# A decode-attention kernel bound by its load stream: the first weight load moved ahead of the opening barrier, the closing barrier dropped, four tiny side loads added

## The chip, the cores and the metric

One core of a Trainium2 chip runs the whole program; the other cores are idle. The metric is the time of one execution in microseconds of device time, the median of several executions. Runs of one experiment alternate on one chip with runs of the kernel before, so a kernel is compared with the kernel before of the same rounds. The profiled span (first to last instruction) is 1.3 to 2.1 us shorter than the time; the rest lies after the last instruction or before the first. A load is shared by 16 DMA engines: "first engine" and "last engine" below are the first and the last of them to land their share. A "packet" is one record of the trace, in the large loads one partition's row. In profile lines, PEld is TensorE's weight load, and a q after an engine's name is the sequencer that issues its instructions.

## The reference, cut to what matters

```python
B, Sq, D = 4, 1, 448
Hq, Hkv, Sk, Dh = 16, 8, 8192, 256          # all bfloat16
# k_cache, v_cache: (4, 8, 8192, 256), 134 MB each

x  = A_x
xn = _layernorm(x)
s  = attention(xn, k_cache, v_cache, wq, wo)  # one query token, 2 query heads per K/V head
g  = silu(_B_ref(xn, w1, w2, w3, w4))         # a small MLP on the same four rows
return x + s * g
```

There are 32 pairs of batch and K/V head ("heads" below). Each needs 4 MB of K and 4 MB of V once, so nearly all of the 279 MB that are read are read once and used once.

## The kernel before: the parts that matter

SyncE (SP) issues the whole load stream on one queue; ScalarE (ACT) issues the small x load.

```python
def prog_sp(sp):
    sp.dma_start(vflat[1][:, 0:DK * HDH], A_wq...).then_inc(S["dwq"], 16)   # 3.67 MB, 28,672 bytes a partition
    sp.dma_start(vflat[0][:, 0:DK * FH],  B_w3...).then_inc(S["dw3"], 16)
    sp.dma_start(w4_sb...,                B_w4...).then_inc(S["dw4"], 16)

    def load_k(h):
        if h >= 2:
            sp.wait_ge(S["v_k"], h - 1)       # K buffer h%2 free: K of body(h-2) is transposed and copied out
        sp.dma_start(kn_dst(h), A_k_cache[b, g]...)                         # 4 MB, 32,768 bytes a partition
    def load_v(h):
        ...
            sp.wait_ge(S["v_v"], h + 1)       # V buffer h%2 free
            sp.dma_start(vflat[h % 2], ...)

    load_k(0)
    load_k(1)
    load_wo(NLATE, HQ, "dwo")                 # 2.75 MB: the last load that waits for no buffer
    for h in range(2, NH):
        load_k(h)                             # load_k(2), "the third K load", waits for body(0)
        load_v(h - 2)
    load_v(NH - 2)
    load_v(NH - 1)                            # in four pieces
    for i, hs in enumerate(LATE):
        load_wo(hs[0], hs[-1] + 1, "dwl%d" % i)   # three late pieces of the output weights, 0.9 MB
    sp.wait_ge(S["v_out"], 1)
    store(sp, 0)
    take(sp, "dout", 16 * NDG)                # wait until the output has landed

def prog_act(act):
    act.dma_start(x_sb[:, :], x2d).then_inc(S["dx"], 16)    # 4 rows of 896 bytes
    ...
```

The prologue is a chain that begins at x: cast to float32, two layernorms (VectorE), transposes, the query projection with wq, the MLP with w3 and w4, then 14 warm-up matmuls (TensorE). Only then TensorE begins body(0):

```python
for i in range(NWARM):                        # NWARM = 14
    pe.matmul(psv[0:PVW, 0:QW], pT[:, 0, 0:PVW], wq_sb[:, 0, 0:QW], start=True, stop=True)
... body(0): transposes of K 0, scores, ...   # its last copied transpose frees the K buffer for load_k(2)
```

Ahead of all this the framework puts four constants on GpSimd and a barrier over all engines, and a barrier closes the program.

Of the kernel before, what the change touches and what calls it, by code (L numbers as in the profile page):

```python
# [10 lines left out]
BF16 = dt.bfloat16  # L11
# [6 lines left out]
class _Chain:  # L18
# [9 lines left out]

    def sync(self):
        self.eng.wait_ge(self.sem, self.n)  # L30


def bass_recurrent_scan__gqa_block_cached__mixer_s_mlp__decode_kernel(
# [12 lines left out]
):  # L46
    Bn, Sq, D = A_x.shape
    _, HKV, SK, DH = A_k_cache.shape
    HD = A_wq.shape[1]
    HQ = HD // DH  # L50
# [3 lines left out]
    NHF = 2  # L54
    DK = D * NHF // P
    assert D * NHF == DK * P and DK % 2 == 1 and D == DK * (P // 2)
    HDH, FH = HD // NHF, F // NHF
# [11 lines left out]
    NH = Bn * HKV  # L69
# [30 lines left out]
    def where(h):  # L100
        return Bn - 1 - h // HKV, h % HKV

    with ExitStack() as es:
        def sb(name, shape, dty):
            return es.enter_context(nc.sbuf_tensor(name, shape, dty))
# [43 lines left out]
        bout = sb("bout", [DP, DQ], F32)  # L149
        out_b = sb("out_b", [DP, DQ], BF16)  # L150
        st = sb("st", [Bn, 16], F32)

        pst = [es.enter_context(nc.psum_tensor("pst%d" % i, [P, 512], F32)) for i in range(NST)]
        psc = [es.enter_context(nc.psum_tensor("psc%d" % i, [P, 512], F32)) for i in range(2)]
# [1 line left out]
        psv = es.enter_context(nc.psum_tensor("psv", [P, 512], F32))  # L156

        S = {n: es.enter_context(nc.semaphore(n)) for n in (
            ["dx", "dwq", "dw3", "dw4", "dwo", "dk0", "dk1", "dv0", "dv1", "dout"]
            + ["dvl%d" % i for i in range(NPIECE)] + ["dwl%d" % i for i in range(len(LATE))]  # L160
            + ["p_td", "p_ta", "p_sc", "p_m1", "p_m2", "p_m3", "p_tr", "p_ou", "p_pv", "p_x", "p_q", "p_h", "p_h2", "p_o"]
            + ["v_ev", "a_ev", "v_rmax", "v_diag", "v_neg", "v_ot", "a_exp", "g_q", "g_c",
# [3 lines left out]
        vflat = [vb[:, i].rearrange("p c d -> p (c d)") for i in range(2)]  # L166
# [17 lines left out]
        def kn_dst(h):  # L184
            return kn[:, h % 2].rearrange("p c d -> p (c d)")

        def store(eng, i):
            eng.dma_start(out2d[:, i * DQ:(i + 1) * DQ], out_b[i * PQ:i * PQ + Bn, :]
                          ).then_inc(S["dout"], 16)

        def prog_sp(sp):
            sp.dma_start(vflat[1][:, 0:DK * HDH],
                         A_wq.rearrange("d (t n) -> (d t) n", t=NHF).rearrange(
                             "(p j) n -> p (j n)", j=DK)).then_inc(S["dwq"], 16)
            sp.dma_start(vflat[0][:, 0:DK * FH],
                         B_w3.rearrange("d (t n) -> (d t) n", t=NHF).rearrange(
                             "(p j) n -> p (j n)", j=DK)).then_inc(S["dw3"], 16)
            sp.dma_start(w4_sb.rearrange("p a k n -> p a (k n)"),
                         B_w4.rearrange("(a p k) n -> p a (k n)", a=NHF, k=NFK)
                         ).then_inc(S["dw4"], 16)  # L200

            def load_k(h):
                b, g = where(h)
                if h >= 2:
                    sp.wait_ge(S["v_k"], h - 1)
                sp.dma_start(kn_dst(h), A_k_cache[b, g].rearrange("(p c) d -> p (c d)", p=P)
                             ).then_inc(S["dk%d" % (h % 2)], 16)

            def load_v(h):
                b, g = where(h)  # L210
                src = A_v_cache[b, g].rearrange("(p c) d -> p c d", p=P)
                if h < NH - 1:
                    sp.wait_ge(S["v_v"], h + 1)
                    sp.dma_start(vflat[h % 2], src.rearrange("p c d -> p (c d)")
                                 ).then_inc(S["dv%d" % (h % 2)], 16)
                else:

                    sp.wait_ge(S["v_k"], h)
                    for i in range(NPIECE):
                        lo, hi = PIECES[i], PIECES[i + 1]  # L220
                        sp.dma_start(
                            kn[:, 1 - h % 2, lo:hi, :].rearrange("p c d -> p (c d)"),
                            src[:, lo:hi, :].rearrange("p c d -> p (c d)")
                        ).then_inc(S["dvl%d" % i], 16)

            load_k(0)
            load_k(1)
            wo_src = A_wo.rearrange("(h p c) n -> p h (c n)", p=P, c=NHALF)

            def load_wo(lo, hi, sem):  # L230
                sp.dma_start(wo_sb[:, lo:hi].rearrange("p h c n -> p h (c n)"),
                             wo_src[:, lo:hi]).then_inc(S[sem], 16)

            load_wo(NLATE, HQ, "dwo")
            for h in range(2, NH):
                load_k(h)
                load_v(h - 2)
            load_v(NH - 2)
            load_v(NH - 1)
            for i, hs in enumerate(LATE):  # L240
                load_wo(hs[0], hs[-1] + 1, "dwl%d" % i)
            sp.wait_ge(S["v_out"], 1)
            store(sp, 0)
            take(sp, "dout", 16 * NDG)

        def take(eng, name, n=1):
            eng.wait_ge(S[name], n).then_inc(S[name], -n)  # L247
# [285 lines left out]
        def prog_pe(pe, xn_mark, xn2_mark):  # L533
# [224 lines left out]
            with nc.Fori(0, 2, engines=[e]) as part:  # L758
# [3 lines left out]
                with pe.If(part == 1):  # L762
                    finish()

        block = es.enter_context(nc.Block())
        marks = []

        @block.sync
        def _(eng):
            prog_sp(eng)  # L770
# [13 lines left out]
        @block.tensor  # L784
        def _(pe):
            prog_pe(pe, *marks)


# [26 lines left out]
```

## Time and profile before

| | |
|---|---|
| time | 655.11 us median (654.53 to 656.17, 4 runs) |
| profiled span | 653.1 us |
| bytes read | 278.99 MB, 427 GB/s over the span |

Lines of the profile page of the kernel before. The digits give busy tenths in 40 slices of 16.3 us; the last line is the load queue: packets, MB, share of 16 engines' span.

```profile
span 653.1 us, 22864 instructions
...
PE   1898997988888988888897887898788798888897
...
DMA  8999999999999999999999999999999999999996
GB/s 362 444 421 421 443 421 446 421 444 423 444 423 444 421 446 421 446 421 446 421 443 423 442 425 442 425 442 425 438 429 438 429 438 429 434 434 434 434 424 288
...
q1 hardware_dynamic: 12328, 278.99, 99.3%
...
```

The load queue takes 99.3% of the DMA engines' time; TensorE is busy for 85% of the span. The kernel is bound by its load stream. In the landing records of the trace two heads (16.78 MB) land every 38.73 us, which is 433 GB/s.

The waits of SP, before (who waits, for whom, us in total, times, longest):

```profile
...
SPq L206 <- DVEq L502: 458.8, 30, 38.6
SPq L214 <- DVEq L471: 133.8, 31, 20.2
...
SPq L247 <- SPq L247: 1.1, 1, 1.1
...
SPq L103 <- SPq L103: 0.5, 1, 0.5
```

The first two lines are waits for free buffers, which cost nothing as long as loads are still queued. The line L247 is the wait for the output's landing, and L103 the closing barrier: 0.5 us.

The head of the program, from the timeline of the kernel before (start, duration, engine, line, operation; in brackets the idle time before and what ended it):

```profile
...
0.73 0.58 ACTq L300 DMA_DIRECT2D x_sb<-in_A_x_dram  x1
...
0.74 0.41 SPq L192 DMA_DIRECT2D vb<-in_A_wq_dram  x1
...
2.57 1.97 DVE L373 CAST x_f<-x_sb 4x448 f32<-4x448 bf16 x1 [1.16 <-DMA x_sb<-in_A_x_dram]
...
25.57 4.52 PE L582 MATMUL psv<-vb,pT 128*32 128x512 bf16 x14
...
30.03 1.07 PE L590 MATMUL pst<-ident_b,kn 128*128 128x128 bf16 x16
...
42.56 0.33 SPq L206 DMA_DIRECT2D kn<-in_A_k_cache_dram  x1
...
```

x is issued at 0.73 us and wq at 0.74. The first K load lands at 29.47 us.

The stretches around the third K load, before (stretch, length, busy us and count per engine, granted clock, DMA share, GB/s). Packets are long here, and a share above 1.00 in a short stretch means that they reach over its edge.

```profile
core 0: us, PE busy (x) PEld busy (x) DVE busy (x) ACT busy (x) POOL busy (x), PEclk, DMA share, GB/s
30.00:44.00 14.00, 13.16 (x275) 12.08 (x274) 6.49 (x12) 7.65 (x11) 0.00 (x0) 1.00 0.97 399
44.00:50.00 6.00, 5.96 (x114) 4.68 (x109) 3.43 (x8) 2.70 (x7) 0.19 (x1) 1.00 1.14 478
...
```

### The profile page before, as it was taken

The numbers are of one execution on the slowest core, as the hardware profiler recorded it, in microseconds if no ns is written. First come the engines' busy times: TensorE is split into PE (matmuls) and PEld (weight loads), VectorE is DVE, ScalarE is ACT, GpSimd is POOL, SyncE is SP. The second block draws the span as 40 slices with busy tenths as digits, with TensorE's granted clock in tenths as the row PEclk, the third lists the DMA queues.
The fourth block names the chain that finished last, engine by engine and source line by source line (L and its number), as shares of the span: only waits on it lengthen the run. The fifth ranks groups of instructions, "written<-read, shape, count | busy, mean of one in ns | idle before, by whom it ended". The sixth has DMA issues, their size and how long they took to land. (4 is left out here: it accounts for less than half of the span.)

```text
span 653.1 us, 22864 instructions
## 1 busy us (share of the span) xinstructions
PE 552.8 (85%) x9937; PEld 473.5 (73%) x9937; DVE 276.1 (42%) x589; ACT 256.2 (39%) x364; POOL 13.5 (2%) x77
## 2 busy tenths in 40 slices
PE   1898997988888988888897887898788798888897
PEld 0487886986676887667787775797677688766785
DVE  7443554343344443434443443434344344443442
ACT  4153543443334443323443342444234344332340
POOL 2000000000000000000000000000000000000000
PEclk9798999888789878889987798989779987888999
DMA  8999999999999999999999999999999999999996
GB/s 362 444 421 421 443 421 446 421 444 423 444 423 444 421 446 421 446 421 446 421 443 423 442 425 442 425 442 425 438 429 438 429 438 429 434 434 434 434 424 288
DMA packets 12354, 279.13 MB, mean 427 GB/s; under 512 B 1205, under 2 KB 3257, under 8 KB 3769
## 3 DMA queue, kind: packets, MB, share of 16 engines
q1 hardware_dynamic: 12328, 278.99, 99.3%
q8 instruction: 7, 0.11, 0.1%
q10 hardware_dynamic: 16, 0.01, 0.0%
q14 instruction: 3, 0.02, 0.0%
HBM read 278.99 MB, written 0.00 MB: 427 GB/s over the span
## 5 line engine op out<-in xcount | busy, mean ns | idle before, releaser
L590 PE MATMUL pst<-ident_b,kn 128*128 128x128 bf16 x4096 | 345.8, 238 | 77.8 <-PEq L247 76.0
L297 ACT ACTIVATE kT<-pst 128x1024 bf16<-128x1024 bf16 x224 | 229.5, 1025 | 357.6 <-ACTq L247 356.7
L590 PEld LDWEIGHTS pst<-ident_b,kn 128*128 128x128 bf16 x4096 | 274.7, 108 | 83.4 <-issue 82.9
L295 DVE COPY kT<-pst 128x1024 bf16<-128x1024 bf16 x288 | 197.5, 692 | 260.9 <-DVEq L247 260.9
L602 PE MATMUL psc<-qc,kT 128*128 128x2 bf16 x4096 | 178.0, 164 | 0.8 <-issue 0.8
L602 PEld LDWEIGHTS psc<-qc,kT 128*128 128x128 bf16 x4096 | 156.7, 98 | 29.5 <-issue 29.1
L641 PE MATMUL psv<-vb,pT 128*4 128x512 bf16 x1056 | 86.3, 378 | 0.4 <-issue 0.4
L620 PE MATMUL psm<-sel,po 128*128 128x2 f32 x272 | 36.7, 257 | 0.5 <-PEq L247 0.5
L620 PEld LDWEIGHTS psm<-sel,po 128*128 128x128 f32 x272 | 34.7, 196 | 0.9 <-issue 0.9
L641 PEld LDWEIGHTS psv<-vb,pT 128*4 128x4 bf16 x1056 | 22.2, 82 | 15.4 <-issue 0.9
L454 DVE TENSOR_REDUCE rmax<-psc 128x2 f32<-128x128 f32 x32 | 9.3, 292 | 48.9 <-DVEq L247 48.9
L472 DVE COPY po<-psv 128x512 f32<-128x512 f32 x34 | 23.5, 692 | 3.0 <-DVEq L247 2.3
L459 DVE TENSOR_REDUCE gmax<-psm 2x1 f32<-2x128 f32 x32 | 8.9, 279 | 34.7 <-DVEq L247 34.7
L319 ACT ACTIVATE pT<-psc,negb 128x64 bf16<-128x64 f32 x66 | 20.6, 333 | 5.4 <-ACTq L247 5.4
L614 PEld LDWEIGHTS psm<-diag,ones_f 2*128 2x128 f32 x66 | 13.9, 260 | 6.4 <-issue 5.4
L282 POOL COPY qc<-qT 128x4 bf16<-128x4 bf16 x32 | 6.0, 188 | 583.3 <-DVEq L471 565.8
L614 PE MATMUL psm<-diag,ones_f 2*128 2x2 f32 x66 | 16.6, 319 | 1.1 <-PEq L247 0.9
L319 ACT ACTIVATION_READ_ACCUMULATOR pT<-psc,negb 128x1 f32 x66 | 13.6, 206 | 0.0
L610 PEld LDWEIGHTS psm<-ident_f,rmax 128*2 128x2 f32 x32 | 2.6, 80 | 14.0 <-issue 14.0
L538 PE MATMUL pst<-ident_b,xn_b 4*128 4x4 bf16 x14 | 0.6, 161 | 13.6 <-DVE xn_b L367 8.9
L632 PE MATMUL psm<-rowsum,ones_f 128*128 128x2 f32 x64 | 11.6, 251 | 0.0
L538 PEld LDWEIGHTS pst<-ident_b,xn_b 4*128 4x128 bf16 x14 | 0.5, 98 | 13.6 <-issue 8.9
(101 smaller groups left out, 119.3 us busy)
## 6 DMA issues: line engine op xcount, KB each, us to landing
kn<-in_A_k_cache_dram SPq DMA_DIRECT2D x32, 4096.0 KB, 25.2
vb<-in_A_v_cache_dram SPq DMA_DIRECT2D x31, 4096.0 KB, 30.5
vb<-in_A_wq_dram SPq DMA_DIRECT2D x1, 3584.0 KB, 11.3
vb<-in_B_w_dram SPq DMA_DIRECT2D x2, 1568.0 KB, 16.2
wo_sb<-in_A_wo_dram SPq DMA_DIRECT2D x1, 2688.0 KB, 43.2
kn<-in_A_v_cache_dram SPq DMA_DIRECT2D x1, 2048.0 KB, 24.9
kn<-in_A_v_cache_dram SPq DMA_DIRECT2D x1, 1024.0 KB, 26.9
kn<-in_A_v_cache_dram SPq DMA_DIRECT2D x2, 512.0 KB, 28.0
```

The lines of the kernel that those rows point to most:

```text
L295: engine.tensor_copy(dst, src).then_inc(S["v_ev"], 1)
L297: engine.activation(dst, src, ACT.Copy).then_inc(S["a_ev"], 1)
L319: ins = act.activation(pv_p[:, :, hh], sc[:, :, hh], ACT.Exp, bias=negb[:, s, hh:hh + 1], scale=SCALE, accum_out=rowsum[:, s, hh:hh + 1])
L454: v.tensor_reduce(rmax[:, :], psc[h % 2][:, 0:NCH * REP].rearrange("p (k h) -> p h k", h=REP), AX.X, ALU.max).then_inc(S["v_rmax"], 1)
L459: v.tensor_reduce(gmax[:, :], psm[0:REP, 0:P], AX.X, ALU.max).then_inc(S["v_s"], 1)
L472: v.tensor_copy(po[:, slot], psv[:, 0:CP * DH]).then_inc(S["v_po"], 1)
L590: ins = pe.transpose(dst[:, t * P:(t + 1) * P], kn[:, h % 2, GC * j + kl, half * P:(half + 1) * P], ident_b[:, :])
L602: ins = pe.matmul(psc[h % 2][:, kk * REP:(kk + 1) * REP], kT[:, j % RING, t * P:(t + 1) * P], qc[:, h % 2, half, :], start=(half == 0), st ...
L614: pe.matmul(psm[:, P:P + REP], ones_f[0:REP, :], diag[:, :], start=True, stop=True).then_inc(S["p_m2"], 1)
L620: ins = pe.matmul(dst(dh)[:, 0:width], po[:, slot, i * DH + dh:(i + 1) * DH:NHALF], sel[:, i, 0:width], start=(i == 0), stop=(i == CP - 1))
L632: pe.matmul(psm[:, P + REP:P + 2 * REP], ones_f[:, :], rowsum[:, h % 2, :], start=True, stop=True)
L641: ins = pe.matmul(psv[o:o + CP * REP, 0:CP * DH], pT[:, h % 2, kk * REP:(kk + CP) * REP], src[:, kk:kk + CP, :].rearrange("p c d -> p (c d)"),
```

## The change

The intent: begin the stream earlier by the length of the opening barrier, end the program without the closing barrier, and put four side loads (15 rows of 64 bytes, never used) into the middle of the stream.

```diff
+def begin_ahead(nc, loads):          # moves the named instructions in front of SP's first barrier instruction
+    ...
+    blocks[0].instructions = first[:at] + list(loads) + first[at:]
+
+def drop_end_barrier(nc):
+    nc.main_func.blocks[-1].instructions = []
...
+        aside = sb("aside", [8, 4, 32], BF16)
...
-            sp.dma_start(vflat[1][:, 0:DK * HDH],
-                         A_wq...).then_inc(S["dwq"], 16)
+            ahead.append(sp.dma_start(
+                vflat[1][:, 0:DK * HDH], A_wq...).then_inc(S["dwq"], 16))
...
             for h in range(2, NH):
                 load_k(h)
                 load_v(h - 2)
+                if h == NH // 2 + 4:
+                    for i in range(4):
+                        n = 1 << i
+                        sp.dma_start(aside[0:n, i, :], A_wo[0:n, 0:32]).then_inc(S["das"], 16)
...
             store(sp, 0)
+            sp.wait_ge(S["das"], 64)
             take(sp, "dout", 16 * NDG)
...
+    begin_ahead(nc, [a.ins for a in ahead])
+    drop_end_barrier(nc)
```

## The prediction

> **What bounds the kernel now.** The load stream. The page's DMA part shows 99.3% of 16 engines' span spent in packets of the one load queue, 278.99 MB at a mean 427 GB/s; TensorE is busy 85%, VectorE 42%, ScalarE 39%. In the trace's landing records, two heads (16.78 MB) land every 38.73 us from about 55 us to 628 us, which is 433 GB/s without a gap, and nearly every 32,768-byte packet takes 1,213 ns. The Trainium skill, "DMA: Bandwidth & Descriptors", Specifications, gives 435 GB/s as the fabric ceiling; the trace agrees. SP waits for free buffers (458.8 us for K, 133.8 us for V), but loads land 25 to 30 us (median) after issue against 9.7 us per transfer, so work is always queued. The tail also hangs on the stream: the last weight load's 16 engines land between 647.6 and 649.8 us, the last matmuls end at 650.3, the store is issued at 651.13, and the span ends at 653.1.
>
> So what moves the first packet moves the end.
>
> **First load ahead of the opening barrier.** In the timeline SP's first instruction is at 0.0; the barrier releases SP at 0.66 and the weight load is issued at 0.74, its first packet starting at 1.77. Issued first, it starts about 0.7 us earlier. It takes SP 0.41 us, and the barrier is held by GpSimd's constants until 0.53, so the barrier does not move. The other loads are issued as before. The stream has no later slack to absorb the shift: the first buffer-dependent K load is issued at 42.6 us, 4 us before the queue would run dry. Gain: 0.7 us. The small x load (896-byte packets at 1.7 us) will queue behind 28,672-byte packets, up to about 1 us later; the layernorm chain has slack, since the first K lands at 29.5.
>
> **No closing barrier.** SP's wait for the stores ends at 663.56 on the trace's clock, the last barrier instruction at 664.09: 0.52 us, all on the end of the path. Gain: 0.5 us, unless what follows the program waits in another way.
>
> **Side loads.** Fifteen rows of 64 bytes. By the skill, same page, "Why a DMA increments its semaphore by 16 and not by 1", a DMA of k rows uses the lowest-numbered k engines, so one engine gets four rows, most get one or none; this trace has no engine numbers. A 448-byte packet took 22 ns and a semaphore packet 9 ns, so I estimate at most 4 x 31 = 0.12 us on one engine, likely not the last. Issuing costs SP about 4 x 0.4 us near 402 us, inside a wait that lasts until 419. Cost: 0 to 0.1 us. I see no gain: every engine's large packets are already back to back.
>
> **Prediction.** 655.15 - 0.7 - 0.5 + 0.05 = 654.0 us; 80% range 653.0 to 655.0. Faster by over 2%: 0.01; within 2%: 0.98; slower by over 2%: 0.01.
>
> **Right if** the first load packet starts near 1.0 us, all landings are about 0.7 us earlier to the end, the cadence stays at 38.73 us, the spread of landings over the engines (2.2 us at the end) keeps its size, and nothing but the stores' landing ends the span, near 651.9.
>
> **Wrong if** the early issue delays the barrier or its packets start no sooner; if the side loads cost a stall (a cadence step after 400 us) or change the spread among engines; if what runs after the program takes back the 0.5 us; or if an added instruction fetch lands on the last engine.

## More of the kernel before

The cast of x ends at 4.54. The warm-up matmuls begin at 25.57, body(0) at 30.03, and when its last transpose has been copied SP issues the third K load, at 42.56.

## The result

655.89 us median (655.8 to 656.29, 4 runs), against 655.11 before. The ratio of the means is 1.0011 (95% interval 0.9998 to 1.0024): the same at 2%, as forecast, but the 1.2 us that were to be gained are not there, and the time lies outside the range of 653.0 to 655.0. Ratios are the mean time of one kernel's runs over that of the other's of the same rounds, so not quite the ratio of the medians quoted.

The page of the changed kernel:

```profile
span 654.4 us, 22857 instructions
...
DMA  9999999999999999999999999999999999999996
GB/s 381 450 365 425 432 431 439 435 433 433 433 433 435 433 433 433 433 433 433 433 432 431 435 431 435 435 433 435 431 435 433 435 431 441 427 441 429 437 423 289
...
q1 hardware_dynamic: 12358, 278.99, 99.2%
...
```

The third number of the GB/s line (32.7 to 49.1 us) says it first: 365 GB/s, where before had 421. The timeline of the head, after:

```profile
...
0.00 0.39 SPq L214 DMA_DIRECT2D vb<-in_A_wq_dram  x1
...
0.80 0.57 ACTq L328 DMA_DIRECT2D x_sb<-in_A_x_dram  x1
...
6.74 0.38 DVE L401 CAST x_f<-x_sb 4x448 f32<-4x448 bf16 x1 [5.26 <-DMA x_sb<-in_A_x_dram]
...
28.15 4.83 PE L610 MATMUL psv<-vb,pT 128*32 128x512 bf16 x14
...
32.91 1.07 PE L618 MATMUL pst<-ident_b,kn 128*128 128x128 bf16 x16
...
44.43 0.33 SPq L229 DMA_DIRECT2D kn<-in_A_k_cache_dram  x1
...
```

wq is issued at 0.00 instead of 0.74, as intended. x is issued at 0.80, but its cast begins at 6.74, after 5.26 us of waiting for x to land. Everything behind it is late by 2.6 us: the warm-up begins at 28.15 instead of 25.57 and body(0) at 32.91 instead of 30.03. The third K load is issued at 44.43 instead of 42.56.

Two accidents of the profiled run before blur these differences. x landed 4.2 us later, but its cast only ended 2.6 us later, because in the run before the cast took 1.97 us and here 0.38; what stretched it there is not shown. And body(0) took 15.62 us before and 14.61 here, because TensorE paused in it before (0.84 us idle) and not here; more on this pause below. Without that pause the third K load would have been later by 2.9 us and not by 1.87.

The same stretches, after:

```profile
core 0: us, PE busy (x) PEld busy (x) DVE busy (x) ACT busy (x) POOL busy (x), PEclk, DMA share, GB/s
30.00:44.00 14.00, 14.00 (x247) 11.92 (x246) 5.45 (x12) 7.58 (x11) 0.00 (x0) 1.00 1.00 409
44.00:50.00 6.00, 5.77 (x99) 3.72 (x97) 3.24 (x8) 1.09 (x2) 0.19 (x1) 1.00 0.88 328
...
```

In the stretch from 44 to 50 us the DMA share falls from 1.14 to 0.88. The waits of SP, after:

```profile
...
SPq L229 <- DVEq L530: 459.7, 30, 41.1
SPq L237 <- DVEq L499: 132.4, 31, 18.9
...
SPq L275 <- SPq L275: 1.2, 1, 1.2
SPq L831 <- PEq L831: 0.2, 1, 0.2
```

The closing barrier's line is gone.

Where the time went, from the landing and packet records of the two profiled runs:

| | before, us | after, us | difference |
|---|---|---|---|
| first packet of wq starts | 1.77 | 1.02 | -0.75 |
| packets of x start | 1.69 to 2.17 | 5.03 to 5.29 | +3.2 |
| x has landed | 2.55 | 6.71 | +4.2 |
| cast of x ends | 4.54 | 7.12 | +2.6 |
| last load ahead of the third K: first engine lands | 44.98 | 44.28 | -0.70 |
| third K load is issued | 42.56 | 44.43 | +1.87 |
| idle time of the 16 engines, 44 to 50 us | none | 20.2 (1.26 each) | |
| third K: first engine, last engine lands | 54.65, 56.39 | 55.88, 58.06 | +1.23, +1.67 |
| last K (head 31) has landed | 618.34 | 619.54 | +1.20 |
| body(31), its first transpose to the transpose of its row maxima | 16.15 | 17.05 | +0.90 |
| store is issued | 651.13 | 652.93 | +1.80 |
| last instruction ends | 653.10 | 654.38 | +1.28 |

The gain of the head is there until 44 us, and it is given back, and more, where the third K load comes. There are 1.26 us of idle time per engine, and the first packets of the third K load take 1.2 to 2.5 us instead of 1.21, which is 0.62 us per engine more. Together with the -0.70 that makes +1.18 for the first engine; +1.23 was measured. That the last K comes +1.20 later is not the same number carried through: the last engine is 1.7 us behind up to head 16 and about 1.2 from head 17 on, because there, near 330 us, the kernel before loses 0.4 to 0.5 us on its last engine and the changed one does not. Two instruction fetches run near 330 us in both; why only one loses by it is not shown.

### The profile page after: what moved, and what is told of

It is laid out like the page before. It is cut to its first block, busy times and chain, and to the rows that moved or that the text cites. A ratio compares the mean times of both kernels' runs of the same rounds, so it can differ in the third digit from the quotient of the medians. Undisturbed runs are those within 1.5% of the kernel's fastest.

```text
span 654.4 us, 22857 instructions
## 1 busy us (share of the span) xinstructions
PE 551.3 (84%) x9937; PEld 472.1 (72%) x9937; DVE 274.2 (42%) x589; ACT 255.8 (39%) x364; POOL 13.4 (2%) x77
## 5 line engine op out<-in xcount | busy, mean ns | idle before, releaser
L347 ACT ACTIVATION_READ_ACCUMULATOR pT<-psc,negb 128x1 f32 x66 | 13.6, 206 | 0.0
## 6 DMA issues: line engine op xcount, KB each, us to landing
wo_sb<-in_A_wo_dram SPq DMA_DIRECT2D x1, 2688.0 KB, 43.2
```

The source lines that it names most:

```text
L347: ins = act.activation(pv_p[:, :, hh], sc[:, :, hh], ACT.Exp, bias=negb[:, s, hh:hh + 1], scale=SCALE, accum_out=rowsum[:, s, hh:hh + 1])
```

## The experiments

Theory A, from the two traces: the early weight load puts large packets in front of x, x delays body(0), the third K load comes when the queue has run empty, and a start from empty is paid for the rest of the run. Theory B, the rival: the head and the end gain what was predicted, and the side loads cost the 2 us.

In the runs below "third K" stands for issue and landing of the third K load in the profiled run.

### Each part alone

**The early load alone.** The diff is the change's `begin_ahead` part.

> The kernel before with the first weight load ahead of the opening barrier, and nothing else of the change. Theory A (the early load delays the small x load, and the stream runs dry): x is cast to float32 about 2.5 us later than before (ends near 7.1 us, not 4.5), the first buffer-dependent K load is issued near 44.4 us, not 42.6, the third K lands about 1.7 us later than before although the first weight load lands 0.7 us earlier, and the time is 1.2 to 2.0 us longer: about 656.7. Theory B (the head gains 0.7 us as predicted, and the side loads cost what is missing): third K 0.7 us earlier, time about 654.4.

Measured: 657.08 us median (656.13 to 657.75, 5 runs) against 655.10, ratio 1.0029 (1.0015 to 1.0043). The cast ends at 7.31, third K is issued at 45.82 and lands at 59.26. Of the three parts this one alone costs 1.9 us (0.29% of 655). The stretch from 44 to 50 us of this run:

```profile
...
44.00:50.00 6.00, 5.86 (x113) 3.99 (x113) 2.13 (x6) 0.47 (x1) 0.03 (x1) 1.00 0.67 230
...
```

The DMA share is 0.67. Theory A holds and B falls. That this run is later than the changed kernel's has two parts: body(0) begins 0.4 us later (33.32), and it took 15.59 us here and 14.61 there. The second is not the clock, which is granted in full in both. It is a pause of TensorE of 0.8 us in front of the 81st score matmul of body(0). In all 17 traces this matmul starts no sooner than 2.0 us after the start of a 16,384-byte instruction fetch. In the seven runs where TensorE gets there less than 1.9 us after it (this one and the kernel before among them) it pauses, for 0.3 to 1.1 us; in the other ten it does not pause for more than 0.2. That it waits for its code is inferred from this.

**No closing barrier alone.** The diff is the change's `drop_end_barrier` part.

> The kernel before without its closing barrier, nothing else. Theory A: the span loses 0.5 us and the time beyond the span falls from about 2.0 to about 1.4 us, so about 1.1 us in all: 654.0. Theory B: 0.5 us in all, 654.6. If what follows the program waits in another way: 655.1. The load stream is as before.

Measured: 654.80 us (654.26 to 655.33, 5 runs) against 655.10, ratio 0.9994 (0.9980 to 1.0008). In the trace the program ends 0.04 us after the output's landing, and 0.56 us after it before. The time beyond the span did not fall: 1.80 to 1.87 us, against 1.62 to 1.87. So 0.5 us in the span, as the prediction had it, and my 1.1 us was wrong: dropping the barrier does not explain why the changed kernel has only 1.4 us beyond its span.

**Side loads alone.** The diff is the change's side loads and the wait for them.

> The kernel before with the four side loads, nothing else. Theory A: under 0.1 us, 655.1 to 655.2, and the landings of the K loads after 400 us keep their distance from those of before. Theory B: the side loads cost the missing 2 us: 656.5 to 657, with a step in the landings near 400 us.

Measured: 655.04 us (654.60 to 655.47, 5 runs) against 655.10, ratio 1.0000 (0.9986 to 1.0013). The last K lands at 618.36, against 618.34. The side loads cost nothing in the stream.

### The cause: x behind large packets

**x late, without an early load.** If theory A is right, the same loss must come from a late x in the kernel before.

```diff
 def prog_act(act):
+    act.wait_ge(S["g_c"], NPI)       # GpSimd's first four constants
     act.dma_start(x_sb[:, :], x2d).then_inc(S["dx"], 16)
```

> The kernel before, unchanged but for the small x load, which its engine issues only after GpSimd's first four constants (near 2 us instead of 0.73). Nothing is ahead of the barrier and the end is as before. Theory A: x lands behind the weight load's packets near 6 us, its cast ends 2.5 us or more later than before, body 0 begins near 33 us, the third K load is issued at 44.3 to 46.4 us, after the queue has run empty near 44.7, its first packets take 1.7 to 2.5 us and its landing comes 1.5 to 3 us later; time 656.3 to 658, a loss without any early load. If x has slack, as the prediction had it: 655.1.

Measured: 658.33 us (657.43 to 659.69, 6 runs) against 655.66, ratio 1.0044 (1.0026 to 1.0062). From the timeline of this run:

```profile
...
0.74 0.41 SPq L192 DMA_DIRECT2D vb<-in_A_wq_dram  x1
...
1.88 0.57 ACTq L301 DMA_DIRECT2D x_sb<-in_A_x_dram  x1
...
8.52 0.38 DVE L374 CAST x_f<-x_sb 4x448 f32<-4x448 bf16 x1 [7.11 <-DMA x_sb<-in_A_x_dram]
...
34.71 1.07 PE L591 MATMUL pst<-ident_b,kn 128*128 128x128 bf16 x16
...
46.23 0.33 SPq L206 DMA_DIRECT2D kn<-in_A_k_cache_dram  x1
...
```

x is issued 1.14 us later than wq, its packets begin at 5.95 to 7.08, and the cast begins at 8.52. Third K is issued at 46.23 and lands at 60.12. A delay of 1.15 us in the issue of 3.5 KB costs 2.9 us of 655 (by the ratio; 2.7 in the medians), just above the 656.3 to 658 that were expected.

**x ahead too.** The changed kernel, with x ahead of the barrier on its own engine.

```diff
-    act.dma_start(x_sb[:, :], x2d).then_inc(S["dx"], 16)
+    ahead_x.append(act.dma_start(x_sb[:, :], x2d).then_inc(S["dx"], 16))
...
     begin_ahead(nc, [a.ins for a in ahead])
+    begin_ahead(nc, [a.ins for a in ahead_x], mybir.EngineType.Activation)
```

> The changed kernel with the small x load also issued ahead of the opening barrier, from its own engine, so that it keeps its place in front of the first weight load's packets. Theory A: x lands near 1.5 us, the third K load is issued near 42 us or earlier, the stream does not run dry, all landings are about 0.7 us earlier than before, and the time is about 653.3 (0.7 us from the head and 1.1 us from the end). Theory B (side loads cost): about 655.9, as the changed kernel.

Measured: 653.64 us (653.13 to 654.40, 5 runs) against 655.10, ratio 0.9980 (0.9967 to 0.9994). Third K is issued at 41.96 and lands at 55.73, no engine is idle, and the last K lands 0.89 us earlier than before. But x's packets start at 2.77 to 2.95, not at once: each still waits behind the first wq packet of its engine. Again, on another chip:

> The changed kernel with x ahead too, again, on the chip of the two variants: 1.3 to 1.6 us below before (653.6), 2.9 us beyond the store's issue, no code fetch after the end.

Measured: 655.03 us (654.01 to 655.19, 5 runs) against 655.58, ratio 0.9992 (0.9978 to 1.0005). This expectation missed. Third K was issued at 43.18, too late, and its first packets took up to 2.5 us. x is one large packet late, and that leaves the third K load on the edge.

**x first on SP.** To put x in front of every large packet, SP issues it ahead of wq.

```diff
 def prog_sp(sp):
+    ahead.append(sp.dma_start(x_sb[:, :], x2d).then_inc(S["dx"], 16))
     ahead.append(sp.dma_start(
         vflat[1][:, 0:DK * HDH], A_wq...
 def prog_act(act):
-    act.dma_start(x_sb[:, :], x2d).then_inc(S["dx"], 16)
```

> The changed kernel with the x load issued by SP ahead of the barrier and ahead of the first weight load, instead of by ScalarE's queue after the barrier. Theory A: x's packets start near 1.0 us, ahead of every large packet; the weight load's start near 1.4 us (0.35 us earlier than before, not 0.75); the cast ends at 2 to 3 us; body 0 begins near 30 us, the third K load is issued by 42.7, before the queue runs empty (near 44.3); no idle time; gain 0.35 (head) + 0.9 (end), so 1.2 us below before: 653.9 to 654.4.

Measured: 653.67 us (653.37 to 654.51, 5 runs) against 655.55, ratio 0.9973 (0.9957 to 0.9990). From its timeline, and below it the stretch from 44 to 50 us:

```profile
...
0.00 0.37 SPq L214 DMA_DIRECT2D x_sb<-in_A_x_dram  x1
...
0.42 0.36 SPq L215 DMA_DIRECT2D vb<-in_A_wq_dram  x1
...
1.76 0.37 DVE L401 CAST x_f<-x_sb 4x448 f32<-4x448 bf16 x1
...
30.37 1.05 PE L618 MATMUL pst<-ident_b,kn 128*128 128x128 bf16 x16 [2.07 <-PEq L276]
...
42.07 0.33 SPq L230 DMA_DIRECT2D kn<-in_A_k_cache_dram  x1
...
```

```profile
...
44.00:50.00 6.00, 4.95 (x87) 3.86 (x86) 3.06 (x8) 2.02 (x3) 0.19 (x1) 1.00 1.13 476
...
```

The cast starts at 1.76, body(0) at 30.37 (now it waits for the first K load, which lands at 30.23), and third K is issued at 42.07. The share is 1.13, as before. The gain is larger than the 1.2 us expected; the rounds of the kernel before had one run of 657.69 us. This version beats both kernels: 0.27% below the kernel before, where the changed kernel was 0.1% above it in both of its comparisons (in other rounds).

### The way from x to the empty queue

**A deeper queue.** If the empty queue is the damage, a queue that empties 2.1 us later must heal it with x as late as ever. The three late output-weight loads are issued at the head.

```diff
     load_wo(NLATE, HQ, "dwo")
+    for i, hs in enumerate(LATE):
+        load_wo(hs[0], hs[-1] + 1, "dwl%d" % i)
     for h in range(2, NH):
...
     load_v(NH - 1)
-    for i, hs in enumerate(LATE):
-        load_wo(hs[0], hs[-1] + 1, "dwl%d" % i)
```

> The changed kernel with the three late output-weight loads (0.9 MB, about 2.1 us of stream) issued at the head, right behind the first output-weight load, instead of at the tail. x is as late as in the changed kernel and the third K load is issued near 44.4 us (to 45.9), but the queue now empties near 46.2 us instead of 44.1. Theory A: little or no idle time and no slow first packets; the last load of all lands near 649.0 instead of 651.0; the time is 0.5 to 1.5 us below the changed kernel's, and below the kernel before moved the same way by 0.7 (head) + 0.9 (end) = 1.6 us. If the late x costs in another way than by the empty queue: as the changed kernel.

> Control for the last: the kernel before with the same three loads at the head. No queue runs empty in either, so this costs or gains at the tail only: the work that follows the last V piece (2.8 us before from its landing to the last matmul) now follows the last load of all; about 0.5 us longer than before, 655.6.

> The changed kernel again, on the chip of its variants. Theory A: 0.7 to 1.2 us above before; third K issued after 44 us or, if TensorE's clock was granted more in body 0, less late; first packets of the third K load slow.

Measured on one chip, 6 runs each: kernel before 655.66 (11 runs); changed kernel 656.41 (ratio 1.0010, 0.9993 to 1.0028); before with the deep queue 657.16 (1.0028, 1.0011 to 1.0044); changed with the deep queue 655.72 (1.0005, 0.9987 to 1.0023). With the short queue the change adds 0.75 us in the medians, with the deep one it takes 1.44 away, where 1.6 was expected. In the profiled run of the changed kernel third K was issued at 45.76 with 39.1 engine-microseconds idle; with the deep queue it was issued at 44.80 and none were idle, though some of its first packets were still slow (up to 2.4 us).

How far this goes: the two kernels with the deep queue differ by 1.27 us in the means, with a standard error of 0.43, which is clear; the 0.7 us that the change adds with the short queue are not clear of noise. And in the one profiled run of the changed kernel with the deep queue (656.41, its second slowest of six) the last K landed at 620.37, as in the control (620.39). So the gain of the head shows in the times and not in this trace, although no engine was idle.

The expectation for the control missed: moving the late loads cost 1.5 us, not 0.5. The last K lands 2.05 us later (620.39 against 618.34), and the store follows 32.49 us after that landing, against 32.79. So the tail hangs on body(31) and what follows it, and 2.1 us less to load at the very end gave only 0.3 us back.

**Fewer warm-up matmuls.** Between the late prologue and body(0) stand the 14 warm-up matmuls.

```diff
-    NWARM = 14
+    NWARM = 2
```

> The changed kernel with 2 warm-up matmuls instead of 14 in front of body 0. x is as late as in the changed kernel (packets near 5 us). Theory A: the warm-up no longer stands between the late prologue (ends near 28.4 us) and body 0, which begins near 29.7 (when K 0 has landed) instead of 32.9 and runs its first 3 us at a lower clock; the third K load is issued near 43 to 43.8, about when the queue empties, and most of the loss is gone: 0.5 to 1.3 us below before. If the loss is not carried by the start of body 0: as the changed kernel, 0.7 above before.

> Control: the kernel before with 2 warm-up matmuls. Its third K load is in time already, so it gains nothing from them: the third K load is issued 0 to 1.5 us earlier, the landings after it and the time are as before, within 0.3 us.

> x first on SP and 2 warm-up matmuls. Theory A: no more than x first alone where that one never runs empty, so the same 1.2 us below before, with fewer slow runs: 653.9 to 654.4.

Measured against 655.55 (11 runs) on one chip: the changed kernel with two warm-up matmuls 653.57 (653.32 to 655.05, 5 runs), ratio 0.9971 (0.9955 to 0.9988); the control 656.28 (655.74 to 658.20, 6 runs), ratio 1.0018 (1.0001 to 1.0035); x first on SP with two warm-up matmuls 654.89 (654.41 to 655.25, 5 runs), ratio 0.9989 (0.9973 to 1.0005).

In the changed kernel they can go: body(0) begins at 29.98 instead of 32.91, and the time falls below the kernel before, by more than expected. The one of its runs that was profiled was its slowest (655.05 us), with third K issued at 44.10 and 13.6 engine-microseconds idle, so no trace shows how much less the four faster ones lost. Where x is early the same cut hurts, which I had not expected. Two lines of the control's timeline:

```profile
...
30.46 1.86 PE L590 MATMUL pst<-ident_b,kn 128*128 128x128 bf16 x16 [3.83 <-PEq L247]
...
44.18 0.33 SPq L206 DMA_DIRECT2D kn<-in_A_k_cache_dram  x1
...
```

Its first 16 transposes take 1.86 us instead of 1.07, body(0) takes 16.83 us instead of 15.62 (of which about 1 us is the pause; this run has none), and third K is issued at 44.18. x first on SP suffers the same way: body(0) takes 17.54 us instead of 14.81, and third K is issued at 44.73. The Trainium skill, "TensorE: Matmul & The Clock Gate", Part 1, says that the array starts at half its clock and needs about 3.4 us of work to be let up. The traces agree on the half clock: in the kernel before, the first warm-up matmuls follow each other every 0.43 us and the later ones every 0.22. They do not show a fixed length: the slow spacing lasts 1.7 us in the run without the closing barrier and 5.2 us in the one with x ahead and no side loads.

### All traces together

All profiled runs with the queue of the kernel before, in order of the issue of the third K load. In the last column is the idle time of all 16 engines between 44 and 50 us.

| run | third K issued, us | third K landed, us | idle, engine-us |
|---|---|---|---|
| changed, x ahead too | 41.96 | 55.73 | none |
| changed, x first on SP | 42.07 | 56.24 | none |
| before, side loads | 42.36 | 56.40 | none |
| before, no closing barrier | 42.46 | 56.46 | none |
| before | 42.56 | 56.39 | none |
| x ahead, increments for side loads | 42.62 | 55.96 | none |
| changed, x ahead too (again) | 43.18 | 57.22 | 2.1 |
| changed, 2 warm-ups | 44.10 | 57.67 | 13.6 |
| before, 2 warm-ups | 44.18 | 57.78 | 4.8 |
| changed | 44.43 | 58.06 | 20.2 |
| x ahead, no side loads | 44.54 | 58.04 | 18.6 |
| x first on SP, 2 warm-ups | 44.73 | 58.33 | 17.7 |
| changed, again | 45.76 | 59.52 | 39.1 |
| before, early load alone | 45.82 | 59.26 | 39.6 |
| before, x late | 46.23 | 60.12 | 34.1 |

Up to 42.6 us the landing does not depend on the issue: the stream decides (56.4 us, or 55.7 to 56.2 where it began earlier). From 43.2 us on the landing follows the issue by 13.4 to 14.0 us. In its profiled run the kernel before stands about one microsecond from its bend: its third K load's packets begin at 44.63, and a load needs 1.0 us from issue to first packet, so by estimate it must be issued by 43.6; with an early stream, which empties 0.7 us sooner, by about 42.9.

### What the side loads do

The changed kernel and both runs with x ahead have 1.4 us between span and time, the kernel before 1.77 (mean of nine). Dropping the barrier alone did not do that. Theory C: the side loads matter only as four more instructions in SP's program; without them SP fetches its last block of code after the end, with them inside the stream.

```diff
-                        sp.dma_start(aside[0:n, i, :], A_wo[0:n, 0:32]).then_inc(S["das"], 16)
+                        sp.sem_inc(S["das"], 16)      # second run; in the first, side loads and wait are left out
```

> The changed kernel with x ahead of the barrier too, and without the side loads. Side loads cost nothing on the chip's engines, so the stream is as in the run with x ahead and side loads. Theory C (the side loads matter only as four more instructions in SP's program, which move a fetch of its code from after the end into the stream): the time beyond the store's issue is about 3.3 us instead of 2.9, a fetch of 8,192 bytes shows after the last instruction, and the time is about 0.4 us longer than with side loads: 654.0. If the side loads have no such effect: 653.6.

> The same with four semaphore increments on SP in place of the four side loads (the same number of SP instructions, no data moved). Theory C: as with side loads, 2.9 us beyond the store's issue, no code fetch after the end, 653.6. If it is the data that matters: as without side loads.

Measured against 655.58: without side loads 655.09 us (654.36 to 656.19, 5 runs), ratio 0.9993 (0.9979 to 1.0006); with four semaphore increments 654.47 (654.15 to 655.21, 5 runs), ratio 0.9989 (0.9976 to 1.0003). The totals differ within their intervals, because here too third K was on the edge (44.54 and 42.62). The end of the program is clear. The time beyond the span is 1.83 to 1.91 us in all five runs without side loads and 1.37 to 1.45 in all five with the increments, as with the side loads (1.39 to 1.44). In the trace an 8,192-byte code fetch runs after the last instruction in the first case (at 655.5 us); in the second it runs at 622.8 and none follows the end. So the 64-byte rows do nothing; what counts is their four instructions, with which a code fetch moves and 0.4 to 0.5 us go. With the closing barrier kept, the side loads brought nothing (1.87 to 2.14 us beyond the span), and one fetch after the end remained. That it is the fetch that takes the time, and that it is SP's, is inferred from where it stands; that four instructions of SP (with the wait for them, which the first run lacks too) decide is shown. The Trainium skill, "Runtime: NRT & Kernel Launch", Instruction fetch mechanics, calls the cost of crossing into a new block of code mostly hidden; if the inference is right, the fetch after the end is not hidden here.

## Why the prediction was wrong

**Right.** The load stream bounds the kernel, and most other terms had their size. The first packet came 0.75 us earlier (predicted 0.7). The barrier moved by 0.07 us only (x is issued at 0.80 instead of 0.73). The closing barrier was worth 0.5 us of span. The side loads cost nothing in the stream (predicted 0 to 0.1 us). The cadence stayed (38.73 us, median 38.72 after).

**Wrong: the x load.** The prediction said that it "will queue behind 28,672-byte packets, up to about 1 us later; the layernorm chain has slack, since the first K lands at 29.5". x landed 4.2 us later. I had counted one packet of about 1.06 us; x started when three packets per engine had gone by. The Trainium skill, "DMA: Bandwidth & Descriptors", Queues, rings and completion order, says that an engine takes turns between its queues packet by packet, and that such a packet is a group of descriptors, typically 9 to 17. A record of the trace is a single row, so three rows before x's turn do not contradict the page; no run here shows how rows are grouped. And the chain had no slack: body(0) began 0.5 us after the first K had landed, because prologue and warm-up ended only then. I had looked at the layernorms alone and not followed the chain through the warm-up matmuls to body(0). x late by itself, in the kernel before, costs 2.9 us.

**Wrong: the slack of the stream.** The prediction said that "the first buffer-dependent K load is issued at 42.6 us, 4 us before the queue would run dry". The 4 us were read against the last engine's landing of the load in front (46.67). Most engines finish that load 1.5 us sooner, and a load needs 1.0 us from its issue to its first packet (44.43 to 45.41). By the estimate under the table of all runs the deadline was 43.6, one microsecond away in the profiled run and not four, and 42.9 once the stream is early. An early stream makes this worse, because it empties earlier while body(0) does not end earlier: the gain at the head moves the deadline forward by the 0.7 us that it gains.

**Missing: the price of an empty queue, and two smaller terms.** A start from empty costs more than the gap, because the first packets are slow (0.62 us per engine). The last body took 17.05 us in the profiled run against 16.15, which added 0.6 us. Such lengths (14.6 to 17.4 us from head 2 on) occur in all kernels here, and the profiled runs with the early load alone and with the changed kernel again had 15.98 and 16.07, so this is no effect of the change. And the time beyond the span fell by 0.4 us, through the four added instructions.

The sum: +1.20 at the last K, +0.60 from there to the store, -0.52 for the barrier (these from the two traces) and -0.37 beyond the span (mean of nine runs before), together +0.9 us. Measured: +0.78 in the medians.

What stays open: why the changed kernel with two warm-up matmuls gained 2 us where at most 1.3 was expected, since only its slowest run was profiled; and what varies from run to run in front of the third K load. Two things do: the 14 warm-up matmuls and the way to body(0) take 4.1 to 5.7 us where the first K load has landed by then, as the half clock lasts longer or shorter, and the pause in body(0) adds 0 to 1.1 us. The changed kernel's first profiled run had no such pause and its second had one, which is most of the way from 44.43 to 45.76.

## What to carry to other kernels

Before moving a large load forward, look at which small load it overtakes: the first thing that the longest chain needs should be issued ahead of the first bulk load, not beside it. In a kernel that is bound by a load stream, the deadline that counts is the first load that waits for a buffer; measure its distance from the moment when the queue runs empty, counting from issue to first packet, and remember that an earlier stream brings that moment nearer. A tiny addition may work through its place in the instruction stream and not through what it does; an equal number of idle instructions tells the two apart.

## What the Trainium skill lacked or had wrong

- "DMA: Bandwidth & Descriptors", Queues, rings and completion order: turns are taken packet by packet, but nothing says how long a small load on another queue waits beside a bulk load that is already running. Here 896-byte packets issued 0.8 us after a load of 28,672-byte packets started 4.2 to 4.5 us after their issue, behind three large packets per engine. Issued ahead of it on the same queue they started 0.9 us after their issue.
- The same page, Bandwidth: it has no price for letting a queue of bulk loads run empty. Here the first 32,768-byte packets after a gap took 1.2 to 2.5 us instead of 1.21, and a 4 MB load took 13.4 to 14.0 us from issue to landing.
- The same page, Where 436 GB/s comes from: it says that for loads from HBM the HBM side (about 358 GB/s) binds. With one core running, this stream read 433 GB/s from HBM for over 570 us, near the fabric ceiling of 435 that the page also gives. The sentence by itself is too strong: the note under the page's own table, with 425 for one large load, keeps the 358 for two cores streaming.
- "Runtime: NRT & Kernel Launch", Instruction fetch mechanics: fetches are called mostly hidden. At the end of a program, four more instructions on one engine (and a wait) changed the time beyond the last instruction from 1.83 to 1.91 us to 1.37 to 1.45 us. And TensorE paused for 0.3 to 1.1 us in the middle of dense work in seven of 17 runs, never going on sooner than 2.0 us after the start of a 16,384-byte fetch.
- "TensorE: Matmul & The Clock Gate", Part 1: that the array starts at half clock agrees with the warm-up matmuls (0.43 and then 0.22 us). No page that I found tells how much a steady body varies: the same body took 14.6 to 17.4 us from head 2 on, at granted clocks of 0.89 to 0.91 on average over a run (1.00 in the shortest bodies, 0.81 to 0.83 in the longest).
